# mLSTM cell and leaky-ReLU feed-forward block: q of chunk 1 through four quadrants, x by five plain transposes, two weight combinations at another place

## The chip, the cores and the metric

The kernel runs on one core of a Trainium2 chip. The metric is the device time of one execution in microseconds (us), the median over several runs. A core has a matrix engine (TensorE; in the profile PE for its matmuls and PEld for its weight loads), VectorE (DVE), ScalarE (ACT), GpSimd (POOL) and SyncE (SP, which here only issues DMAs). The engines run side by side, each in its own order, and wait for each other by semaphores. Matmuls read the on-chip memory SBUF and write to the accumulator memory PSUM; GpSimd works on SBUF alone.

## The reference

An mLSTM cell for 4 batches, 8 heads, 768 tokens and a head dimension of 40, whose output of shape (3072, 320) goes through a feed-forward block with 2048 hidden units:

```python
for t in range(S):
    m_new = np.maximum(f_gate[:, :, t] + m, i_gate[:, :, t])
    f_stab = np.exp(f_gate[:, :, t] + m - m_new)
    i_stab = np.exp(i_gate[:, :, t] - m_new)
    m = m_new
    C = f_stab * C + i_stab * np.einsum('bhd,bhe->bhde', vt, kt)
    n = f_stab * n + i_stab * kt
    h_tilde = np.einsum('bhde,bhe->bhd', C, qt)
    denom = np.maximum(np.abs(np.einsum('bhd,bhd->bh', n, qt)), 1.0)
    y[:, :, t] = sigmoid(o_gate[:, :, t]) * h_tilde / denom
x = y.transpose(0, 2, 1, 3).reshape(3072, 320)
h = x @ w_in                      # (3072, 2048)
out = np.maximum(0.01 * h, h) @ w_out
```

## The kernel before

**Tiling.** The 768 tokens are cut into six chunks of 128 (c = 0 to 5), and a step s = 4c + b is one chunk of one batch b with its 8 heads. The recurrence becomes, for each step, a masked score product of k and q inside the chunk and a product of q with the state S carried over. Chunk 0 is computed in its whole length (`u_transpose`, `u_scores`, `u_values`, `gate`). From chunk 1 on each step is cut into two halves of 64 tokens, which lie on partitions 0 to 63 and 64 to 127. The feed-forward block runs in groups g = 0 to 5 of 512 tokens, one chunk of all four batches; group 0 is computed plainly (`ff_units`, tiles `ph` at line 804 and `po` at line 826), the groups from 1 on by a scheme of seven products on sums and differences of blocks of the operands (`fast_firsts` with `ph` at line 977, `fast_units` with `po` at line 861), for which such sums of w_in (`sums_of_weights`), of w_out (`mixed_weights`) and of x (`sums_of_x`) are made once or per group.

**Order of the work.** TensorE, VectorE, ScalarE and GpSimd run in the order in which the program was written out: first `first_chunk`, then a loop over c = 1 to 6, in which the units of feed-forward group c - 1 (index i) are interleaved by hand with the cell units of chunk c: `place` and `pairs` say behind which i a cell unit stands, and single lines such as `if c == 1 and i >= 24: run(sums, 3)` place other work. SyncE issues its DMAs in an order of its own.

**A step of chunk 1** (s = 4 to 7; `u_parts`, then `u_plain`). `u_split` has put k and q, transposed, into `kqT` by way of the PSUM tiles `tk` (line 581), whose matmuls against the identity go through all four pairs of a row half and a column half. `prep_qs` has multiplied q by its gate on GpSimd (`qs`, in a tile named `y`, line 523). `split_qs` transposes `qs` by matmuls against the identity into two PSUM tiles `tq` (line 567): head by head, token half 0 to the upper output rows and token half 1 to the lower. ScalarE copies each tile into `qn` (line 569, 40 partitions x 512). Then come the scores `sd` (line 662) with the state's increments (line 667), VectorE's product with the weights `w` into `qn` (line 672) and its addition to the state S (`state_add`, line 643). `w` is made by ScalarE's exponentials (line 494) of what GpSimd masked (line 486). `u_plain` multiplies `qn` by S into `hN` (line 710); VectorE and GpSimd form x from it (lines 721 and 726), and `ahead` then prepares the next step (`tk`, `qs` by line 523, `vu` by line 514, the next mask).

**x to its transposed form.** In chunks 0 and 1 `u_x` transposes x (128 tokens x 320) into `xT`, which has five slots of 128 partitions, each with two blocks of 64 columns: the slots hold columns 0 to 127, 128 to 255, then the pair of 256 to 319 and 0 to 63, then 64 to 191 and 192 to 319. Four slots come from transposes of 128 columns (tile `xt`, line 789); the middle one from two matmuls of 64 columns against the identity, one for each half of the output rows (tile `xe`, line 791). Three copies bring them to `xT` (lines 792 to 794). In chunk 0 the last copy of every second step is VectorE's (`on_v`). Chunk 0's x comes from `gate` (lines 695 and 699), and between its steps stand GpSimd's memsets of `prepare_step` (lines 178 to 180) and the widening of w_in from 64-bit words (`narrow_weights`, lines 272 to 281). From chunk 2 on x goes through DRAM (`u_mix`, `x_dr`, `gather_x`) and does not pass `u_x`.

**Gates.** `gates(c)` runs short scans on VectorE over 32 rows; from chunk 1 on it subtracts the running maximum from the input gate into a tile `il` of its own (lines 299 and 300). `load_fi` brings the gates of a later chunk into one of two buffers `fi`.

**Combinations of w_out.** `mixed_weights` makes four combinations of quarters of w_out on VectorE, one per `next` (lines 224 to 227): t3 = a22 - a12, then a12 is overwritten by a12 - a11, then t2 and t4 from that. They are used by `fast_units` of group 1 for the first time (units 14 and up): t4 by p4, t2 by p6, t3 by p7, a12 by p5. The first two stand at the end of group 0, the other two in group 1 at i = 11 and 12. In group 1 units 0 to 13 are those of `fast_firsts`; p5's bank is used further by p3.

Of the kernel before, what the change touches and what calls it, by code (L numbers as in the profile page):

```python
# [19 lines left out]
def kernel(  # L20
# [28 lines left out]
    P = 128  # L49
# [6 lines left out]
    D1 = D + 1  # L56
    QW = 32
    DB = D // 2
    V1 = DB + 1
    TB = P // QW  # L60
    SL = P // 2
# [228 lines left out]
    def gates(c):  # L290


        m0 = m0s.get(c)
        n = P if c == 0 else BH
        fc, il = (f0[:], i0[:]) if c == 0 else (fi[c][:, 0, :], fi[c][:, 1, :])
        F = wk.tile([n, P], F32, name="F", bufs=1)
        nc.vector.tensor_tensor_scan(F[:], fc, zeros[:n].to_broadcast([n, P]), 0.0, op0=ALU.add, op1=ALU.add)
        if c > 0:
            il_t = wk.tile([BH, P], F32, name="il", bufs=1)
            nc.vector.tensor_scalar(il_t[:], il, scalar1=m0[:], scalar2=None, op0=ALU.subtract)  # L300
            il = il_t[:]
        m = wk.tile([n, P], F32, name="m", bufs=1)
        nc.vector.tensor_tensor_scan(m[:], fc, il, -1e30 if c == 0 else 0.0, op0=ALU.add, op1=ALU.max)
        a = early[:, 2, :] if c == 0 else wk.tile([n, P], F32, name="a", bufs=1)
        nc.vector.tensor_tensor(a[:], F[:], m[:], op=ALU.subtract)
        bu = wk.tile([n, 3, P], F32, name="bu", bufs=1)
        nc.vector.tensor_tensor(bu[:, 0, :], il, F[:], op=ALU.subtract)
        if c + 1 < NB:
            m1 = wk.tile([BH, 1], F32, name="m0")
            if c == 0:  # L310
                nc.vector.tensor_copy(m1[:], m[:BH, P - 1 :])
            else:
                nc.vector.tensor_tensor(m1[:], m0[:], m[:, P - 1 :], op=ALU.add)
            m0s[c + 1] = m1
        if c > 0:
            na = wk.tile([BH, 1], F32, name="na")
            nc.vector.tensor_tensor(na[:], m[:, SL - 1 : SL], F[:, SL - 1 : SL], op=ALU.subtract)
        bus[c] = bu, a, (na if c > 0 else None)
# [243 lines left out]
    def split_qs(s):  # L562

        tq = [psc.tile([P, H, SL], F32, name=f"tq{u}", tag="c") for u in range(2)]
        for h in range(H):
            for u, toks, rows in subs(s):
                nc.tensor.matmul(tq[u][rows, h, :], lhsT=st[s]["qs"][toks, h], rhs=ident[toks, toks], start=True, stop=True)  # L567
        for u, toks, rows in subs(s):
            nc.scalar.copy(mixed(s)[rows, u], tq[u][rows])

    def u_split(s):

# [117 lines left out]
    def gate(s):  # L690

        d = st[s]
        d["x"] = wk.tile([P, Dm], F32, name="x")
        x3 = d["x"][:].rearrange("p (h d) -> p h d", d=D)
        nc.vector.scalar_tensor_tensor(
            x3, in0=d["o"].rearrange("p (h d) -> p h d", d=D), scalar=1.0, in1=d["pa"][:, :, :D],
            op0=ALU.add, op1=ALU.mult,
        )
        nc.vector.tensor_tensor(x3, x3, d["den"][:].unsqueeze(2).to_broadcast([P, H, D]), op=ALU.mult)

    def u_plain(s):

# [11 lines left out]
        state_next(s, 1)  # L714
        den = wk.tile([P, H], F32, name="den")
        denominators(den[:], hN[:, :, 0, DB])
        if b < 2:
            d["x"] = wk.tile([P, Dm], F32, name="x")[:]
        else:
            d["x"] = wk.tile([P, H, D1], F32, name="hn")[:].rearrange("p h d -> p (h d)")[:, :Dm]  # L720
        nc.vector.scalar_tensor_tensor(
            d["x"].rearrange("p (n d) -> p n d", d=DB), in0=natural(s, 2).rearrange("p h (k d) -> p (h k) d", d=DB), scalar=1.0,
            in1=hN[:].rearrange("p h k d -> p (h k) d")[:, :, :DB], op0=ALU.add, op1=ALU.mult,
        )
        x3 = d["x"].rearrange("p (h d) -> p h d", d=D)
        nc.gpsimd.tensor_tensor(x3, x3, den[:].unsqueeze(2).to_broadcast([P, H, D]), op=ALU.mult)
        state_add(s, 1)

    def u_mix(s):
# [48 lines left out]
    def u_x(s, last=None):  # L778

        c, b = divmod(s, B)  # L780
        d = st[s]
        if b == 0:
            st["xT", c] = wk.tile([P, KC, GT], F32, name="xT", bufs=1)
        xT = st["xT", c]
        xt = psc.tile([P, KC - 1, P], F32, name="xt", tag="c")
        xe = psc.tile([P, P], F32, name="xe", tag="c")
        x, tok = d["x"], ts(b, P)
        for n, at in enumerate((0, P, DP, DP + P)):
            nc.tensor.transpose(xt[:, n, :], x[:, at : at + P], ident[:])  # L789
        for r, at in enumerate((KF * P, 0)):  # L790
            nc.tensor.matmul(xe[ts(r, DP), :], lhsT=x[:, at : at + DP], rhs=ident[:], start=True, stop=True)
        nc.scalar.copy(xT[:, :2, tok], xt[:, :2, :])  # L792
        nc.scalar.copy(xT[:, 2, tok], xe[:])
        (last or nc.scalar.copy)(xT[:, 3:, tok], xt[:, 2:, :])
        if c > 0:
            del st[s]

# [418 lines left out]
    with tc.manual_schedule(engines={E.PE, E.DVE, E.Activation, E.Pool}):  # L1216
# [20 lines left out]
        late = {}  # L1237
        masks = {0: (2, 3), 14: (4, 5)}
        pairs = (1, 1, 3, 3, 13, 13, 17, 17, 17)
        sums = sums_of_weights()  # L1240
        N1 = 14
        now = (None for n in range(2, QN + NF // 2) for _ in narrow_weights(n))
        chores, slow = [], []
        for c in range(1, NB + 1):
# [6 lines left out]
            for i in range(n_ff):  # L1251
# [20 lines left out]
                        del fine[min(fine)]  # L1272
                if c == 1 and i >= 24:
                    run(sums, 3)
                if c == 1 and i == n_ff - 2:
                    mixes = mixed_weights()
                if c == 1 and i >= n_ff - 2 or c == 2 and 11 <= i < N1 - 1:
                    next(mixes)
                if i == n_ff - 1 and c < NB:
                    sums_of_x(c)  # L1280
# [74 lines left out]
```

## Time and profile before

| | |
|---|---|
| runs, us | 490.13, 490.45, 492.2 (median 490.45) |
| the profiled execution, us | 489.68 |
| its span, first to last instruction, us | 487.9 |
| mean granted clock of TensorE | 0.983 |
| TensorE's matmuls busy | 476.3 (98%) |
| VectorE busy | 334.8 (69%) |
| ScalarE busy | 202.8 (42%) |
| GpSimd busy | 176.3 (36%) |

In the profile L567 is line 567 of the kernel before; a group of instructions is named by its line, engine, operation, output and inputs. An fp32 matmul against weights shows as two records, a transpose as one. A window's row gives the stretch, its length, then busy time and instructions of PE, PEld, DVE, ACT and POOL, then the granted clock of TensorE (1.00 is full speed), the share of the DMA engines and GB/s. In a row of a timeline stand start, duration, engine, line, operation, shapes and count, and in brackets how long the engine had been idle and what is inferred to have released it.

### The profile page before, as it was taken

Reading aid. Unit: us, or ns where it says so; the run is one execution under the profiler, and the core shown is the slowest. Engines: PE = TensorE matmul, PEld = TensorE weight load, DVE = VectorE, ACT = ScalarE, POOL = GpSimd, SP = SyncE. Lnnn points to the kernel's source line nnn. Section 1 sums busy time; section 2 is a strip of 40 time slices with the busy share of each in tenths; the row PEclk is TensorE's granted clock in tenths of the full one; section 3 lists DMA queues with packets and bytes.
Section 4 is the critical chain, followed back from the end, with each engine's and each line's share of the span. In section 5 each row is a group of like instructions: output and inputs, shape, how many; then the busy total and the mean of one; then the engine's idle time right before and its main releaser. Section 6 shows DMA issues by size and latency. Waiting matters only on the chain.

```text
span 487.9 us, 14080 instructions
## 1 busy us (share of the span) xinstructions
PE 476.3 (98%) x5685; PEld 428.5 (88%) x5685; DVE 334.8 (69%) x557; ACT 202.8 (42%) x488; POOL 176.3 (36%) x233
## 2 busy tenths in 40 slices
PE   8798999999999999999999999999999999999997
PEld 6676998777678899989899988899989899988997
DVE  3756567699999798888687878688647677104631
ACT  3662498864335631256420345520346411153210
POOL 4311305552376222785113784113773003700020
PEclk9887899999999999999999999999999999999999
DMA  9999686878651584675763775764865212100001
GB/s 122 172 200 210 121 223 179 207 138 173 145 142 28 126 170 83 148 167 122 173 137 88 172 150 123 181 124 90 174 146 126 60 48 68 68 1 1 1 0 55
DMA packets 165040, 59.31 MB, mean 122 GB/s; under 512 B 128560, under 2 KB 155760, under 8 KB 164976
## 3 DMA queue, kind: packets, MB, share of 16 engines
q1 hardware_dynamic: 124944, 51.23, 47.3%
q10 hardware_dynamic: 40032, 7.18, 9.0%
q8 instruction: 45, 0.74, 0.6%
q14 instruction: 19, 0.16, 0.1%
HBM read 51.68 MB, written 6.70 MB: 120 GB/s over the span
## 4 chain that ended last, share of the span: by engine, by line
PE 90%; DMA 4%; SPq 4%; DVE 1%; issue 1%; ACTq 0%; ACT 0%
PE ph L977 32%; PE po L861 32%; PE po L826 7%; PE ph L804 7%; SPq L91 4%; PE pT L740 3%; PE sd L662 3%; DMA acts<-in_moe_w_in_dram 2%; DMA raw<-in_moe_w_in_dram 1%; PE sd L667 1%; PE hN L710 1%; PE tk L581 1%; PE tq L567 1%; PE xt L789 1%; DMA f<-in_f_gate_dram 0%
## 5 line engine op out<-in xcount | busy, mean ns | idle before, releaser
L861 PE MATMUL po<-w_out,acts 128*128 128x160 f32 x640 | 89.1, 300 | 0.0
L861 PEld LDWEIGHTS po<-w_out,acts 128*128 128x128 f32 x640 | 87.3, 190 | 0.6 <-ACT acts L1002 0.3
L977 PE MATMUL ph<-xT,w_in 64*128 64x256 f32 x720 | 82.7, 378 | 0.0
L977 PEld LDWEIGHTS ph<-xT,w_in 64*128 64x128 f32 x720 | 69.3, 187 | 8.8 <-issue 1.1
L1006 DVE TENSOR_TENSOR acts<-acts,ph 128x512 f32<-128x512 f32 x60 | 38.4, 683 | 43.4 <-PE ph L977 43.4
L861 PE MATMUL po<-raw,acts 128*128 128x160 f32 x480 | 66.4, 300 | 0.0
L861 PEld LDWEIGHTS po<-raw,acts 128*128 128x128 f32 x480 | 65.4, 190 | 0.3
L1010 ACT COPY acts<-ph 128x512 f32<-128x512 f32 x60 | 32.1, 586 | 49.1 <-PE ph L977 49.1
L639 POOL TENSOR_TENSOR S<-S,f 40x336 f32<-40x336 f32 x36 | 29.5, 819 | 61.2 <-PE pT L740 26.2
L1002 ACT ACTIVATE acts<-acts 128x1024 f32<-128x1024 f32 x30 | 31.7, 1056 | 44.1 <-DVE acts L1006 33.7
L486 POOL TENSOR_TENSOR w<-w,i 128x512 f32<-128x512 f32 x20 | 26.7, 1340 | 59.5 <-DMA w<-a_dr 41.3
L494 ACT ACTIVATE w<-w,gT 128x64 f32<-128x64 f32 x160 | 41.7, 339 | 10.5 <-DMA w<-a_dr 5.7
L804 PE MATMUL ph<-xT,w_in 64*128 64x256 f32 x320 | 38.5, 395 | 0.7 <-DVE w_in L281 0.7
L672 DVE TENSOR_TENSOR qn<-w,sd 64x512 f32<-64x512 f32 x40 | 27.3, 683 | 15.6 <-ACT acts L1010 4.5
L826 PE MATMUL po<-w_out,acts 128*128 128x320 f32 x128 | 37.1, 441 | 0.0
L977 PE MATMUL ph<-acts,w 64*128 64x256 f32 x320 | 36.6, 381 | 0.0
L804 PEld LDWEIGHTS ph<-xT,w_in 64*128 64x128 f32 x320 | 32.5, 196 | 4.4 <-PE dC L619 0.8
L754 POOL TENSOR_TENSOR xb<-xb,den 128x320 f32<-128x320 f32 x16 | 11.6, 727 | 61.1 <-DVE xb L751 61.1
L977 PEld LDWEIGHTS ph<-acts,w 64*128 64x128 f32 x320 | 30.4, 187 | 3.7
L826 PEld LDWEIGHTS po<-w_out,acts 128*128 128x128 f32 x128 | 23.5, 190 | 9.8 <-issue 1.0
L959 POOL TENSOR_TENSOR acts<-xT 64x256 f32<-64x256 f32 (+1 forms) x30 | 25.5, 862 | 13.0 <-ACT xT L792 9.9
L894 POOL TENSOR_TENSOR y<-y,raw 128x160 f32<-128x160 f32 x10 | 9.4, 944 | 55.8 <-DVE acts L896 45.3
(173 smaller groups left out, 780.0 us busy)
## 6 DMA issues: line engine op xcount, KB each, us to landing
rb<-in_k_dram SPq DMA_DIRECT2D x64, 80.0 KB
rb<-in_q_dram SPq DMA_DIRECT2D x64, 80.0 KB
rb<-in_o_gate_dram SPq DMA_DIRECT2D x64, 80.0 KB
ea<-a_dr SPq DMA_DIRECT2D x32, 128.0 KB
raw<-in_moe_w_out_dram SPq DMA_DIRECT2D x6, 640.0 KB
w<-a_dr ACTq DMA_DIRECT2D x24, 128.0 KB
xT<-x_dr SPq DMA_DIRECT2D x32, 96.0 KB
x_dr<-x SPq DMA_DIRECT2D x64, 40.0 KB
```

Source lines behind the costliest of these rows:

```text
L486: nc.gpsimd.tensor_tensor(w, w, cm2.unsqueeze(1).to_broadcast([P, H, SL]), op=ALU.add)
L494: yield nc.scalar.activation(w[:, h, :], w[:, h, :], AF.Exp, bias=gT[c][:, 0, bh : bh + 1], scale=1.0)
L639: nc.gpsimd.tensor_tensor(new, old, g, op=ALU.mult)
L672: nc.vector.tensor_tensor(mixed(s)[toks, u], w[toks], bank[1 - u][toks], op=ALU.mult)
L804: nc.tensor.matmul(ph[r][:, cols], lhsT=w_row(r, slot, j), rhs=xT[DP * r : DP * (r + 1), slot, cols], start=(slot == 0), stop=(slot == KC ...
L826: nc.tensor.matmul(po[n][:], lhsT=acts[:, f, ts(n, P)], rhs=w_out[:, f, :], start=(f == 0), stop=(f == NF - 1),)
L861: nc.tensor.matmul(bank[:], lhsT=left[:, f, :], rhs=right[:, f, :], start=f == 0, stop=f == KH - 1)
L959: nc.gpsimd.tensor_tensor(to, left, right, op=ALU.subtract)
L977: nc.tensor.matmul(bank[r][:, e, :], lhsT=left(r)[rows, e], rhs=right(r)[rows], start=first and e == 0 and m == 0, stop=e == 1 and m == le ...
L1002: nc.scalar.activation(to, z, AF.Prelu, alpha=0.01)
L1006: nc.vector.tensor_tensor(to[:, 2 * r : 2 * r + 2], to[:, 2 * r : 2 * r + 2], bank[r], op=ALU.add)
L1010: nc.scalar.copy(to[:, 2 * r : 2 * r + 2], bank[r])
```

## The change

Five edits come together:

1. `split_qs` takes the heads in the order 0, 4, 1, 5, 2, 6, 3, 7. Heads 0 to 3 go to the output rows they went to; heads 4 to 7 go to the other half. Each row half of the array is so used with both column halves. Four ScalarE copies of 256 columns bring the tiles to `qn` in place of two of 512.
2. `u_x` makes five transposes of 128 columns: two into `low`, three into `high`. So that the middle slot (columns 256 to 319 and 0 to 63) is one run of 128 columns, x gets a width of 384 (`XW`), and GpSimd copies its first 64 columns behind the 320, in `gate` (chunk 0) and in `u_plain` (chunk 1). Two copies per step bring the tiles to `xT`.
3. In chunk 0 this copy of step s stands on GpSimd's queue where `gate(s)` is written out, that is, ahead of the memsets of `prepare_step`.
4. The first two of the four combinations of w_out move from the end of group 0 to i = 3 and 4 of group 1.
5. The input gate is scaled in place in `fi`; the tile `il` is gone.

On TensorE, VectorE, ScalarE and SyncE the order of all other instructions stays as it was.

```diff
--- before.py
+++ after.py
@@ -56,6 +56,7 @@
     D1 = D + 1
     QW = 32
     DB = D // 2
+    XW = Dm + DP
     V1 = DB + 1
     TB = P // QW
     SL = P // 2
@@ -296,9 +297,7 @@
         F = wk.tile([n, P], F32, name="F", bufs=1)
         nc.vector.tensor_tensor_scan(F[:], fc, zeros[:n].to_broadcast([n, P]), 0.0, op0=ALU.add, op1=ALU.add)
         if c > 0:
-            il_t = wk.tile([BH, P], F32, name="il", bufs=1)
-            nc.vector.tensor_scalar(il_t[:], il, scalar1=m0[:], scalar2=None, op0=ALU.subtract)
-            il = il_t[:]
+            nc.vector.tensor_scalar(il, il, scalar1=m0[:], scalar2=None, op0=ALU.subtract)
         m = wk.tile([n, P], F32, name="m", bufs=1)
         nc.vector.tensor_tensor_scan(m[:], fc, il, -1e30 if c == 0 else 0.0, op0=ALU.add, op1=ALU.max)
         a = early[:, 2, :] if c == 0 else wk.tile([n, P], F32, name="a", bufs=1)
@@ -562,11 +561,13 @@
     def split_qs(s):
 
         tq = [psc.tile([P, H, SL], F32, name=f"tq{u}", tag="c") for u in range(2)]
-        for h in range(H):
+        for h in (0, 4, 1, 5, 2, 6, 3, 7):
             for u, toks, rows in subs(s):
-                nc.tensor.matmul(tq[u][rows, h, :], lhsT=st[s]["qs"][toks, h], rhs=ident[toks, toks], start=True, stop=True)
+                to = rows if h < 4 else slice(SL * u, SL * u + D)
+                nc.tensor.matmul(tq[u][to, h, :], lhsT=st[s]["qs"][toks, h], rhs=ident[toks, toks], start=True, stop=True)
         for u, toks, rows in subs(s):
-            nc.scalar.copy(mixed(s)[rows, u], tq[u][rows])
+            for hs, to in ((slice(0, 4), rows), (slice(4, H), slice(SL * u, SL * u + D))):
+                nc.scalar.copy(mixed(s)[rows, u, hs], tq[u][to, hs])
 
     def u_split(s):
 
@@ -690,13 +691,14 @@
     def gate(s):
 
         d = st[s]
-        d["x"] = wk.tile([P, Dm], F32, name="x")
-        x3 = d["x"][:].rearrange("p (h d) -> p h d", d=D)
+        x = d["x"] = wk.tile([P, XW], F32, name="x")[:]
+        x3 = x[:, :Dm].rearrange("p (h d) -> p h d", d=D)
         nc.vector.scalar_tensor_tensor(
             x3, in0=d["o"].rearrange("p (h d) -> p h d", d=D), scalar=1.0, in1=d["pa"][:, :, :D],
             op0=ALU.add, op1=ALU.mult,
         )
         nc.vector.tensor_tensor(x3, x3, d["den"][:].unsqueeze(2).to_broadcast([P, H, D]), op=ALU.mult)
+        nc.gpsimd.tensor_copy(x[:, Dm:], x[:, :DP])
 
     def u_plain(s):
 
@@ -714,16 +716,14 @@
         state_next(s, 1)
         den = wk.tile([P, H], F32, name="den")
         denominators(den[:], hN[:, :, 0, DB])
-        if b < 2:
-            d["x"] = wk.tile([P, Dm], F32, name="x")[:]
-        else:
-            d["x"] = wk.tile([P, H, D1], F32, name="hn")[:].rearrange("p h d -> p (h d)")[:, :Dm]
+        x = d["x"] = wk.tile([P, XW], F32, name="x" if b < 2 else "hn")[:]
         nc.vector.scalar_tensor_tensor(
-            d["x"].rearrange("p (n d) -> p n d", d=DB), in0=natural(s, 2).rearrange("p h (k d) -> p (h k) d", d=DB), scalar=1.0,
+            x[:, :Dm].rearrange("p (n d) -> p n d", d=DB), in0=natural(s, 2).rearrange("p h (k d) -> p (h k) d", d=DB), scalar=1.0,
             in1=hN[:].rearrange("p h k d -> p (h k) d")[:, :, :DB], op0=ALU.add, op1=ALU.mult,
         )
-        x3 = d["x"].rearrange("p (h d) -> p h d", d=D)
+        x3 = x[:, :Dm].rearrange("p (h d) -> p h d", d=D)
         nc.gpsimd.tensor_tensor(x3, x3, den[:].unsqueeze(2).to_broadcast([P, H, D]), op=ALU.mult)
+        nc.gpsimd.tensor_copy(x[:, Dm:], x[:, :DP])
         state_add(s, 1)
 
     def u_mix(s):
@@ -778,20 +778,15 @@
     def u_x(s, last=None):
 
         c, b = divmod(s, B)
-        d = st[s]
         if b == 0:
             st["xT", c] = wk.tile([P, KC, GT], F32, name="xT", bufs=1)
-        xT = st["xT", c]
-        xt = psc.tile([P, KC - 1, P], F32, name="xt", tag="c")
-        xe = psc.tile([P, P], F32, name="xe", tag="c")
-        x, tok = d["x"], ts(b, P)
-        for n, at in enumerate((0, P, DP, DP + P)):
-            nc.tensor.transpose(xt[:, n, :], x[:, at : at + P], ident[:])
-        for r, at in enumerate((KF * P, 0)):
-            nc.tensor.matmul(xe[ts(r, DP), :], lhsT=x[:, at : at + DP], rhs=ident[:], start=True, stop=True)
-        nc.scalar.copy(xT[:, :2, tok], xt[:, :2, :])
-        nc.scalar.copy(xT[:, 2, tok], xe[:])
-        (last or nc.scalar.copy)(xT[:, 3:, tok], xt[:, 2:, :])
+        x, xT, tok = st[s]["x"], st["xT", c], ts(b, P)
+        low = psc.tile([P, 2, P], F32, name="xt", tag="c")
+        high = psc.tile([P, KC - 2, P], F32, name="xe", tag="c")
+        for t, n, at in ((low, 0, 0), (low, 1, P), (high, 1, DP), (high, 2, DP + P), (high, 0, 2 * P)):
+            nc.tensor.transpose(t[:, n, :], x[:, at : at + P], ident[:])
+        nc.scalar.copy(xT[:, :2, tok], low[:])
+        (last or nc.scalar.copy)(xT[:, 2:, tok], high[:])
         if c > 0:
             del st[s]
 
@@ -1237,7 +1232,7 @@
         late = {}
         masks = {0: (2, 3), 14: (4, 5)}
         pairs = (1, 1, 3, 3, 13, 13, 17, 17, 17)
-        sums = sums_of_weights()
+        sums, mixes = sums_of_weights(), mixed_weights()
         N1 = 14
         now = (None for n in range(2, QN + NF // 2) for _ in narrow_weights(n))
         chores, slow = [], []
@@ -1272,9 +1267,7 @@
                         del fine[min(fine)]
                 if c == 1 and i >= 24:
                     run(sums, 3)
-                if c == 1 and i == n_ff - 2:
-                    mixes = mixed_weights()
-                if c == 1 and i >= n_ff - 2 or c == 2 and 11 <= i < N1 - 1:
+                if c == 2 and i in (3, 4, 11, 12):
                     next(mixes)
                 if i == n_ff - 1 and c < NB:
                     sums_of_x(c)
```

## The prediction

> **What bounds the kernel now.** First the page's head: span, and busy times of the engines.
>
> ```profile
> span 487.9 us, 14080 instructions
> PE 476.3 (98%) x5685; PEld 428.5 (88%) x5685; DVE 334.8 (69%) x557; ACT 202.8 (42%) x488; POOL 176.3 (36%) x233
> ```
>
> TensorE is busy 98% of the span. Then the chain of waits in order of time (start, us, what, records):
>
> ```profile
> 44.75 0.50 DVE x L699
> ...
> 47.34 1.41 DVE w_in L281
> ...
> 48.88 10.46 PE ph L804 x80
> 59.34 1.03 PE tk L581 x64
> 60.37 6.73 PE ph L804 x60
> 67.10 0.96 PE tq L567 x30
> ...
> 116.01 1.06 PE hN L710 x32
> 117.08 2.35 PE po L826 x8
> 119.43 0.44 PE xt L789 x4
> 119.86 0.37 PE xe L791 x4
> ...
> 484.87 0.32 DVE y L920
> ```
>
> Up to 48.88 other engines and DMA decide; the last to release TensorE there is VectorE's widening of w_in (L281). From 48.88 to 484.87 every piece of the chain is TensorE behind itself. So a microsecond taken out of TensorE behind 48.88 shortens the kernel by one, unless an operand is then late; before 48.88 only what delays L281, and the clock, count.
>
> **The change, part by part.** *tq in four quadrants (chunk 1, four steps).* Now 30 records take 0.96, 32 ns each, and the last two run among those of sd. The neighbour tk has 64 records of the same shape in 1.03, 16 ns each, and its order alternates two row halves and two column halves as the new order of tq does (heads 0, 4, 1, 5 and so on). At tk's pitch 32 records take 0.515. I count 0.99 for them now: a gain of 0.475 a step, 1.9 in all. Bounds: 0 (nothing more overlaps) to 4 x 0.51 = 2.0.
>
> [...]
>
> *x by five plain transposes (chunk 1, four steps).* Four transposes take 0.44, 0.11 each, and the two half-width matmuls 0.37. Five will take 0.55 in place of 0.81: 0.26 a step, 1.04 in all. Bounds: 0.9 to 1.1, as all parts of it are there. Only the fifth reads the 64 columns that GpSimd now copies behind x. In steps 4 to 6 x is ready long before 119.43; for step 7 it comes just ahead of the S addition at 123.03 (a row below), and its transposes are at 119.43 + 3 x (0.81 + 4.70) = 136. The copy, at most a 512-column memset's 0.52 (below), stands on GpSimd's queue ahead of the next y, which tq needs, and of vu, which sd needs. I cost it at nothing, since the ph or po between (6.73 ahead of the first tq) covers it and GpSimd is busy 36%; with that cover gone it would be 3 x 0.25 to 0.5. ScalarE copies xT in two pieces instead of three.
>
> *What hands time back in chunk 1.* TensorE reaches hN of step 7 (116.01) 4 x 0.475 = 1.9 earlier, at 114.11. hN needs the state S from L643. ScalarE and VectorE in steps 6 and 7:
>
> ```profile
> 88.86 2.37 ACT L587 COPY kqT<-tk 40x512 f32<-40x512 f32 x4 [1.16 <-PE tk L581]
> ...
> 95.41 1.18 ACT L569 COPY qn<-tq 40x512 f32<-40x512 f32 x2
> 96.49 0.59 ACT L494 ACTIVATE w<-w,gT 128x64 f32<-128x64 f32 x2
> ```
> ```profile
> 97.11 1.40 DVE L672 TENSOR_TENSOR qn<-w,sd 64x512 f32<-64x512 f32 x2 [3.65 <-DMA rb<-in_o_gate_dram]
> ...
> 114.69 0.50 DVE L643 TENSOR_TENSOR S<-S,sd 40x336 f32<-40x336 f32 x1
> ...
> 123.03 0.51 DVE L643 TENSOR_TENSOR S<-S,sd 40x336 f32<-40x336 f32 x1
> ```
> ```profile
> 97.10:115.20 18.10, 18.10 (x247) 13.31 (x246) 17.39 (x28) 10.35 (x22) 9.15 (x8) 1.00 0.81 158
> ```
>
> From 97.11 on VectorE is full (third pair of the last row: 17.39 of 18.10), and S of step 7 ends at 115.19. It can move up only as far as L672 of step 6 does. The DMA named there isn't what holds L672: it starts at 97.11 where w's exponentials end (96.49 + 0.59), and those close a chain on ScalarE that began behind tk of step 6. That tk moves up by two savings, 0.95. Four copies of 256 columns in place of two of 512 cost ScalarE between nothing and another 1.18; by columns it is nothing but the start-up, so I take 0.15. So S ends 0.8 earlier, and hN waits 115.19 + 0.06 - 114.11 - 0.8 = 0.35. Bounds: 0, and 1.4 where S doesn't move and GpSimd's copies slow VectorE too. The next meeting is xt of step 5 with S at 123.54: from the first meeting VectorE needs 8.35 and TensorE some 8.6 (119.86 + 0.37 + twice 2.35, less 0.26, from 116.01), so no second wait.
>
> *Two combinations of w_out moved from the end of group 0 to units 3 and 4 of group 1.*
>
> ```profile
> 136.77 1.49 DVE L224 TENSOR_TENSOR raw<-w_out 128x1280 f32<-128x1280 f32 x1
> 138.30 1.90 DVE L225 TENSOR_TENSOR w_out<-w_out 128x1280 f32<-128x1280 f32 x1
> ...
> 145.15 1.38 DVE L672 TENSOR_TENSOR qn<-w,sd 64x512 f32<-64x512 f32 x2 [0.96 <-PE sd L667]
> ...
> 166.60 1.28 DVE L1006 TENSOR_TENSOR acts<-acts,ph 128x512 f32<-128x512 f32 x2 [2.33 <-PE ph L977]
> ```
> ```profile
> 168.92 5.35 PE L977 MATMUL ph<-xT,raw 64*128 64x256 f32 x48
> ```
>
> They take 3.39. At their old place VectorE had 0.96 to spare ahead of L672, and TensorE will come 2.5 earlier: left there, L672 would be some 1.5 late; taken away, it still waits for sd. At the new place VectorE waits 2.33 ahead of p5's additions. The cover falls short by 1.06, so the additions end at 168.94 instead of 167.88, counted in the old times; p3, which writes on into p5's banks from 168.92, needs the first of them, 0.6 before that. Cost 0; where the additions run slower, up to 0.5. Ahead of them, hb of u_mix comes 1.5 later; its x is for group 2. The gate scaled in place adds no instruction; the next load into it waits for one more reader.
>
> *Chunk 0.* Here TensorE waits, so its 0.26 a step isn't counted. VectorE's copy of three blocks replaces a wait for ScalarE and a copy of two: even. But GpSimd's queue now has the copy of x(3), whose x ends at 45.25, ahead of prepare_step's six memsets, which ended at 43.07. They will run from about 45.5 to 48, under L281:
>
> ```profile
> 42.55 0.52 POOL L180 MEMSET S<- 32x512 f32 x1
> ```
> ```profile
> 47.25 1.48 DVE L281 CUSTOM_DVE_ANT_0 w_in<-acts,w_in 128x2560 uint16<-128x2560 uint16 x1
> ...
> 60.39 2.59 DVE L281 CUSTOM_DVE_ANT_0 w_in<-raw,w_in 128x2560 uint16<-128x2560 uint16 x1
> ```
> ```profile
> 21.00:28.00 7.00, 5.51 (x26) 3.89 (x28) 6.25 (x9) 4.35 (x13) 0.00 (x0) 0.52 1.21 194
> 42.00:52.00 10.00, 7.66 (x64) 6.12 (x66) 7.68 (x19) 1.55 (x5) 0.77 (x2) 0.50 0.84 169
> ```
>
> The same L281 took 2.59 at 60.39, where GpSimd's mask addition ran beside it. So its end moves by 0 to 1.1; I take 0.3, as the memsets read nothing and cover less than half of it. Up to 52 TensorE runs at half clock (granted clock 0.50 in the last row), where a delay costs half of itself: 0.15, less 0.05 for the first two x. That is 0.1; bounds -0.2 and 1.1.
>
> *Sum*: -1.9 - 1.04 + 0.35 + 0.1 = -2.5. The profiled execution took 489.68 (span 487.9), which gives 487.2. The runs shown are 490.13, 490.45 and 492.2; their median is 0.77 above the profiled one, and I add 0.5 of that: **487.7**.
>
> **Rivals.** *A, all of it arrives*: VectorE's work moves up with TensorE and hN never waits: -2.94, and chunk 0 even, 486.7 + 0.5 = 487.2. For it: step 6 is gated by ScalarE, not by a load. Against: 17.39 of 18.10.
>
> *B, VectorE paces chunk 1*: S of step 7 doesn't move, hN waits 1.4, and p3 waits 0.5: -2.94 + 1.4 + 0.5 + 0.1 = -0.9, 489.3. For it: VectorE full from 97 on. Against: step 6's start at the end of w.
>
> *D, the change doesn't do what it says*: the quadrants overlap no further, only x gains, and hN has nothing to wait for: -1.04 + 0.1 = -0.9, 489.2. Against: tk.
>
> *C, the clock, on the other side.* The two half-clock rows above cover 7 and 10 us. 80 records from 48.88 took 10.46; at full clock (6.73 for 60) they would take 8.97, so 3.1 us of half clock cost 1.49, 0.48 each. The change takes plain matmuls out of both stretches and delays ph at 48.88. If each stretch lasts half as long again, 8.5 us more cost 4.1, and with L281's full 1.1 the loss is 5.2 against a gain of 2.6: +2.6, 492.3 + 0.5 = 492.8. It decides from 5 us of additional half clock on. For it: in the second row TensorE was busy for 7.66 of 10.00 and still at half clock. Against: most of that work stays.
>
> [...]
>
> **How the numbers follow.** Forecast 0.48 (own range 486.7 to 488.7), A 0.17, B 0.08, D 0.05, C 0.22. 0.5% (2.45 us, about what a measurement of this kernel can tell from no change) below the median is 488.0, above it 492.9. Faster: A and 0.7 of the forecast, 0.51. Slower: the upper part of C, 0.14, as its price has no ceiling in these rows. Within: the rest, 0.35. The range 486.2 to 491.0 leaves out most of C and little below A.
>
> **What would show it.** Right: tq near 0.52 a step, xt and xe together 0.55, ph again released near 49, hN of step 7 with a wait under 1, L672 in group 1 still waiting for sd. Wrong: tq still near 0.96 (D); TensorE waiting for S or for L1006 by more than 1 (B); granted clock 0.50 well beyond 52, or L281 at 2 us and more (C).

## The result and the profile after

The changed kernel takes 489.69 us (median of 22 executions, 487.42 to 490.37) against 490.55 us (22 executions, 489.52 to 496.98) of the kernel before on the same chips: a ratio of 0.9968, 95% interval 0.9954 to 0.9982. That is a gain of 1.6 us by the ratio, where 2.5 had been forecast. A ratio leaves out executions more than 1.5% above the fastest of their kernel. The profiled execution took 487.76 us. Its line numbers are those of the changed kernel: ph of group 0 is L799, tq L567, tk L582, hN L712, S L644, x's transposes L787.

The 22 executions are not one group: nine lie between 487.4 and 488.9 (below, the lower group) and thirteen between 489.35 and 490.4 (the upper group). The mean granted clock was 0.976 in ten of the thirteen and in none of the nine (there 0.979 or 0.982). As an estimate from these means, spread over the span of 486 and with half clock as the only lower state (in the windows of 1 us of the changed kernel's trace, 20 to 60, the clock is 0.50 or 1.00 but for one window at an edge of a stretch), 0.982 means 17 us at half clock, 0.979 means 20 and 0.976 means 23. The profile below is one of the nine, and what it shows is not the whole of the median.

The head of its page, and the line of the page that gives the chain's shares by engine:

```profile
span 486.0 us, 14033 instructions
PE 471.8 (97%) x5661; PEld 426.0 (88%) x5661; DVE 334.1 (69%) x557; ACT 202.8 (42%) x488; POOL 180.2 (37%) x241
...
PE 82%; DMA 7%; SPq 6%; DVE 2%; ACT 1%; issue 1%; POOL 0%; ACTq 0%; POOLq 0%
```

The chain of waits of the changed kernel (start, us, what, records):

```profile
46.51 1.41 DVE w_in L282
...
48.06 7.52 PE ph L799 x40
...
78.16 1.23 POOL S L640
...
79.47 1.19 POOL vu L513
...
95.45 5.51 DMA rb<-in_q_dram
...
101.01 1.09 PE tk L582 x60
...
109.64 0.59 PE tq L567 x32
...
115.76 1.06 PE hN L712 x32
116.82 2.35 PE po L821 x8
119.17 0.22 PE xt L787 x2
119.39 0.33 PE xe L787 x3
119.72 4.31 PE po L821 x16
...
136.44 5.38 PE ph L972 x48
...
482.94 0.32 DVE y L915
```

Up to tk of step 7 the chain is no longer TensorE alone: it runs over GpSimd's vu, over loads of k, and over the load of q for step 7, which lands at 100.96 and releases tk. Behind that it is TensorE again. The single pieces came out as meant: tq 0.59 a step (0.96 before), x 0.22 + 0.33 = 0.55 (0.81 before), and po behind x 4.31 for 16 records, where it was 4.50.

Where the time came from and went, by the starts of TensorE's groups or of the chain's pieces in the two traces (before, then after):

| | before | after | difference in it |
|---|---|---|---|
| ph released at the end of chunk 0 | 48.88 | 48.06 | -0.82 |
| its 80 records | 10.46 | 11.80 | +1.34 |
| tq to the next ph or po, steps 4, 5, 6, 7 | 1.95, 1.96, 1.96, 1.95 | 1.52, 1.64, 1.89, 1.62 | -0.43, -0.32, -0.07, -0.33 |
| hN of step 6 to the next po | 2.10 | 2.46 | +0.36 |
| x of step 4 to group 1 | 19.08 | 17.27 | -1.81 |
| group 1 to the last y | 346.36 | 346.50 | +0.14 |

The differences sum to -1.94; the last y starts 1.93 earlier (484.87, 482.94).

Windows of the changed kernel at the end of chunk 0 (stretch, length, busy time and count of PE, PEld, DVE, ACT, POOL, then granted clock, DMA share, GB/s):

```profile
41.00:44.00 3.00, 1.01 (x9) 0.77 (x8) 2.63 (x7) 0.81 (x2) 0.24 (x1) 0.95 1.19 194
44.00:47.00 3.00, 2.38 (x37) 2.08 (x37) 1.52 (x3) 0.37 (x1) 2.19 (x7) 0.50 1.06 235
...
50.00:53.00 3.00, 3.00 (x18) 2.58 (x16) 1.02 (x5) 0.30 (x2) 0.00 (x0) 0.50 0.72 147
53.00:56.00 3.00, 3.00 (x26) 2.77 (x24) 0.00 (x0) 0.74 (x4) 2.44 (x3) 0.84 0.75 98
```

ph starts earlier but runs at half clock to nearly 54, where it was 52 before, and so ends later. GpSimd's six memsets ran from 44.71 to 47.03, most of them ahead of the widening of w_in (46.43 to 47.91): only their last 0.6 us ran beside it, and it took 1.41 as before.

### The profile page after: what moved, and what is told of

It reads as the page before. It is cut to its first block, busy times and chain, and to the rows that moved or that the text cites. A ratio compares the mean times of both kernels' runs of the same rounds, so it can differ in the third digit from the quotient of the medians.

```text
span 486.0 us, 14033 instructions
## 1 busy us (share of the span) xinstructions
PE 471.8 (97%) x5661; PEld 426.0 (88%) x5661; DVE 334.1 (69%) x557; ACT 202.8 (42%) x488; POOL 180.2 (37%) x241
## 4 chain that ended last, share of the span: by engine, by line
PE 82%; DMA 7%; SPq 6%; DVE 2%; ACT 1%; issue 1%; POOL 0%; ACTq 0%; POOLq 0%
PE ph L972 33%; PE po L856 32%; SPq L92 6%; PE po L821 6%; PE pT L740 3%; DMA kn<-in_k_dram 3%; PE sd L663 3%; PE ph L799 3%; DMA acts<-in_moe_w_in_dram 1%; DMA rb<-in_q_dram 1%; PE sd L668 1%; DMA qn<-in_q_dram 1%; DMA w<-a_dr 1%; DVE w_in L281 1%; DVE w_in L282 1%
## 5 line engine op out<-in xcount | busy, mean ns | idle before, releaser
L640 POOL TENSOR_TENSOR S<-S,f 40x336 f32<-40x336 f32 x36 | 31.0, 862 | 58.0 <-PE pT L740 25.4
L997 ACT ACTIVATE acts<-acts 128x1024 f32<-128x1024 f32 x30 | 31.7, 1056 | 43.1 <-DVE acts L1001 35.4
L799 PE MATMUL ph<-xT,w_in 64*128 64x256 f32 x320 | 39.7, 403 | 1.6 <-DVE w_in L282 1.6
L673 DVE TENSOR_TENSOR qn<-w,sd 64x512 f32<-64x512 f32 x40 | 27.3, 683 | 16.4 <-ACT w L493 8.7
L799 PEld LDWEIGHTS ph<-xT,w_in 64*128 64x128 f32 x320 | 33.5, 200 | 5.6 <-ACT kqT L599 1.2
```

The costliest lines, as they stand in the source:

```text
L640: nc.gpsimd.tensor_tensor(new, old, g, op=ALU.mult)
L673: nc.vector.tensor_tensor(mixed(s)[toks, u], w[toks], bank[1 - u][toks], op=ALU.mult)
L799: nc.tensor.matmul(ph[r][:, cols], lhsT=w_row(r, slot, j), rhs=xT[DP * r : DP * (r + 1), slot, cols], start=(slot == 0), stop=(slot == KC ...
L997: nc.scalar.activation(to, z, AF.Prelu, alpha=0.01)
```

## Experiments

Times are medians with their range and number; the ratio is to the kernel before on the same chip. Line numbers are those of each kernel.

### The parts alone

tq's order alone, in the kernel before (`e1_tq`: the hunk of `split_qs` from the diff, nothing else).

> The kernel before with the four-quadrant order of tq alone. Theory (tq's saving arrives in part: 0.43 + 0.32 + 0.07 + 0.33 at its four places in the changed kernel, less 0.36 where tk of step 7 waits for its load of q): 490.5 - 0.8 = 489.7, up to 490.5 - 1.15 = 489.4, all executions within 0.8 us of each other, as chunk 0 is that of before. Rival D (the quadrants bring the tq row but nothing behind it): 490.5. Rival by the prediction's own term (1.9 less a wait of 0.35): 489.0.

Measured: 489.5 (488.33 to 492.22, 12 executions), ratio 0.9981 (0.9965 to 0.9997). In its trace TensorE goes from the second run of ph (60.84, before 60.30) to group 1 (138.03, before 138.44) 0.95 faster. So the gain is there, at half the size of the term of 1.9. The four pieces from tq to the next ph or po take 1.53, 1.61, 1.53 and 1.61 here, 1.54 less than before in all; most of the rest of it is handed back in a wait of 0.41 for VectorE's hn (L723). The first half-clock stretch of this trace lasted 10.2 us (18.7 to 28.9) and in the kernel before 6.8, although chunk 0 is the same in both.

The transposes of x alone, with the gate scaled in place to make room (`e2_x`: the hunks of `gates`, `gate`, `u_plain` and `u_x`).

> The kernel before with x by five transposes alone, in chunks 0 and 1. Theory: chunk 1 gives back 1.81 (0.26 a step in xt and xe and 0.19 a step in the po behind them); chunk 0 hands back 0.52 where the clock rises as in the profile of the changed kernel, and 2.7 where it stays low for some 6 us more: two groups of times, near 489.2 and near 491.4. Rival (chunk 0 costs nothing, the 0.52 and the two groups come from elsewhere): one group near 488.7. Rival (the prediction's 1.04 for chunk 1): 489.5.

Measured: 492.63 (492.0 to 493.08, 5 executions), ratio 1.005 (1.0038 to 1.0063): slower than before, and worse than each theory. Two windows of its trace:

```profile
26.00:29.00 3.00, 2.22 (x11) 1.73 (x11) 1.96 (x2) 1.17 (x2) 0.77 (x2) 0.50 1.07 238
29.00:32.00 3.00, 3.00 (x16) 2.58 (x15) 0.00 (x0) 0.00 (x0) 0.00 (x0) 0.50 1.24 211
```

In the kernel before, the clock was back by 28.2 and the first 20 records of ph took 2.64 there. Here it stays at half to about 32, and they take 4.56 (at 27.67). That is chunk 0's loss: ph of the end starts at 50.59. In chunk 1 the 1.81 does arrive. From the start of group 1 (139.41) to the end of its ph run it then takes 37.5, where the kernel before takes 35.8 (138.44 to 174.20). There the two combinations of w_out still stand at the end of group 0 in this kernel. The next but one experiment takes that up.

### Chunk 0 as before, all else changed

In the changed kernel, `u_x` of chunk 0 keeps the four transposes, the two half-width matmuls and the three copies, and `gate` has no copy on GpSimd.

```diff
@@ def gate(s):
-        nc.gpsimd.tensor_copy(x[:, Dm:], x[:, :DP])
@@ def u_x(s, last=None):
+        if c == 0:
+            xt = psc.tile([P, KC - 1, P], F32, name="xt", tag="c")
+            xe = psc.tile([P, P], F32, name="xe", tag="c")
...
+            return
```

> The changed kernel with x of chunk 0 transposed as before (four transposes and two half-width matmuls, no copy on GpSimd), everything else changed. Theory (chunk 0 is where 0.52 and the upper group of times come from): 490.5 - 2.6 = 487.9, one group of times, mean granted clock as before, 80 ph records from about 48.9 in 10.5. Rival (the spread of the times has another origin, in chunk 1 or in the loads): two groups as in the changed kernel, median 489.7 less at most 0.5.

Measured: 487.46 (486.98 to 487.98, 5 executions), ratio 0.9945 (0.9933 to 0.9957), all below the upper group, mean clock 0.979 to 0.982. ph starts at 48.72 and its 80 records take 10.38. With chunk 0's part gone the other parts bring 2.7 us by the ratio, so that part costs the changed kernel 1.1 us in the ratio, and without it none of five executions came into the upper group, where thirteen of 22 were.

### The two combinations of w_out back at their old place

In e9_old0, the loop's lines as before:

```diff
-                if c == 2 and i in (3, 4, 11, 12):
+                if c == 1 and i == n_ff - 2:
+                    mixes = mixed_weights()
+                if c == 1 and i >= n_ff - 2 or c == 2 and 11 <= i < N1 - 1:
```

> e9_old0 with the two combinations of w_out at the end of group 0, as before the change. Theory (the prediction's step): TensorE comes 2.5 earlier to group 1, VectorE had 0.96 to spare there, so the first additions of group 1 on VectorE are 1.5 late and TensorE waits up to that: 487.5 + 1.0 to 1.5 = 488.5 to 489.0. Rival (TensorE has other work between, the move is worth nothing): 487.5, no wait of TensorE for VectorE between 135 and 152.

Measured: 490.14 (488.76 to 494.05, 10 executions), ratio 0.9995 (0.9976 to 1.0014). VectorE's timeline at the start of group 1:

```profile
138.64 1.92 DVE L225 TENSOR_TENSOR raw<-w_out 128x1280 f32<-128x1280 f32 x1
140.60 1.90 DVE L226 TENSOR_TENSOR w_out<-w_out 128x1280 f32<-128x1280 f32 x1
142.42 0.94 DVE L298 TENSOR_TENSOR_SCAN F<-fi,zeros 32x128 f32<-32x128 f32 x1
...
146.53 1.38 DVE L673 TENSOR_TENSOR qn<-w,sd 64x512 f32<-64x512 f32 x2
```

and TensorE's waits in that stretch (who, for whom: us in total, times, longest):

```profile
PE pT L739 <- DVE S L644: 1.3, 2, 0.7
```

The changed kernel's row at the same place:

```profile
143.08 1.39 DVE L673 TENSOR_TENSOR qn<-w,sd 64x512 f32<-64x512 f32 x2 [1.22 <-PE sd L668]
```

Here L673 starts 3.4 later than in the changed kernel, while TensorE reaches group 1 only 0.5 later (136.84 against 136.37). From the start of group 1 to the end of its ph run it takes 37.9 (136.84 to 174.73), in e9_old0 35.8 (135.89 to 171.65): 2.1 lost. (In this trace ph's 80 records took 11.79, with the same chunk 0 as e9_old0 and its 10.38; from that, from pa ahead of it, 4.21 in place of 3.77, and from the mean clock of 0.979 the second half-clock stretch is estimated at 13.7 us. That loss is not in the 2.1.) The kernel before, with the same old place, takes 35.8 as well. So the move is worth about 2 us once x is faster; in the kernel before nothing is lost there. Moving the two combinations alone, in the kernel before, was not tried.

### The clock at the start of chunk 0: filling 0.78 us

In the changed kernel TensorE idles 0.78 from 26.5 on, ahead of the first ph (the row at 27.29 in the next section); before the change it did not. Ahead of the transposes of step 2's q were put two matmuls of the identity, then instead three transposes of it:

```diff
+            if s == 2 and i == 1:
+                for _ in range(2):
+                    nc.tensor.matmul(tp[:, 0, :], lhsT=ident[:], rhs=ident[:], start=True, stop=True)
```
```diff
+            if s == 2 and i == 1:
+                for _ in range(3):
+                    nc.tensor.transpose(tp[:, 0, :], ident[:], ident[:])
```

> The changed kernel with two extra 128x128 matmuls on the identity (their output is overwritten) ahead of the transposes of step 2's q, so that TensorE no longer idles 0.78 ahead of the first ph at 27.2. Theory (that idle time, which x by five transposes opened, keeps the clock at half for one more stretch of some 3.4 us in most executions, and the 20 ph records take 4.56 in place of 2.43): all executions have a mean clock of 0.979 to 0.983, one group of times, median 488.0 (the lower group of the changed kernel) and up to 0.5 less. Rival (the clock's stretches begin and end by chance): median 489.7 and two groups as in the changed kernel.

> The changed kernel with three extra 128x128 transposes of the identity at the same place, for about the same time. If transposes are busy time for the clock as matmuls are: the same as with the two matmuls, one group near 488.0. [...]

Measured: with matmuls 487.34 (486.08 to 488.53, 6 executions), ratio 0.9931 (0.9911 to 0.995), mean clock 0.979 to 0.982, all below the upper group. In its trace the first ph took 2.95 for 20 records in place of 2.43, so half clock reached some 1.1 into it; with the mean clock of 0.979 and ph's 80 records at the end of chunk 0 (10.69) the first half-clock stretch is estimated at 10.2 us (19.0 to 29.3). With transposes 488.68 (486.36 to 491.58, 12 executions), ratio 0.9965 (0.9944 to 0.9986), mean clock 0.975 or 0.976 in five of the twelve, all of these above 489.8. None of six with matmuls against five of twelve with transposes is weak evidence of a difference between the two, and the profiled execution with transposes, the slowest of the twelve, lost its time elsewhere. Its chain of waits:

```profile
96.60 6.74 DMA rb<-in_q_dram
...
103.39 1.86 PE tk L582 x60
105.24 3.20 PE po L824 x8
```

and a window of it:

```profile
103.00:107.00 4.00, 3.61 (x64) 2.87 (x65) 2.95 (x6) 1.65 (x3) 3.04 (x4) 0.57 0.87 164
```

The load of q for step 7 landed at 103.3 and not at 101. TensorE waited 2.8, the clock fell, tk and po then ran at half clock (1.86 for 1.09, 3.20 for 2.35), and hN of step 6 to the po behind it took 6.00 in place of 2.10: a price of 3.9 us for a load that is 2.4 late. So an execution can be slow in two ways, and times alone don't say which it was. Whether some of the changed kernel's thirteen are of this kind stays open, as none of them was traced; but e9_old0, which comes to that load 0.75 earlier, has none in its five.

### Plain matmuls for transposes

To see whether transposes keep the clock low, the five transposes of x in chunk 0 of the changed kernel were made plain matmuls on the identity:

```diff
+            if c == 0:
+                nc.tensor.matmul(t[:, n, :], lhsT=x[:, at : at + P], rhs=ident[:], start=True, stop=True)
+            else:
                 nc.tensor.transpose(t[:, n, :], x[:, at : at + P], ident[:])
```

> The changed kernel with the five transposes of x in chunk 0 (20 in all) as plain matmuls on the identity, nothing added. [...]

Measured: 489.74 (485.23 to 492.73, 12 executions), ratio 0.997 (0.9943 to 0.9997). The median is that of the changed kernel (489.69), the clock is not: its mean reached 0.993 in the three fastest, which no kernel with transposes in all four steps of chunk 0 did (at most 0.989, in e5_swap), and was 0.976 in two of those above 491. Two windows:

```profile
47.00:50.00 3.00, 3.00 (x28) 2.77 (x30) 0.52 (x2) 0.37 (x1) 2.10 (x7) 0.51 1.04 179
50.00:53.00 3.00, 1.85 (x36) 1.76 (x34) 2.88 (x7) 0.00 (x0) 0.00 (x0) 1.00 0.51 117
```

By windows of 1 us the stretch lasted from 43.1 to 50.0, 6.8 us; in the changed kernel 43.7 to 54.0, 10.2. But in this execution half clock came once more between (36.3 to 39.7), under the second ph of chunk 0 (4.11 for 20 records, 2.43 before). And plain matmuls take longer, five of them 2.27 at half clock (x of step 0, 22.70 to 24.97) where five transposes took 1.23 (22.27 to 23.50): ph of the end of chunk 0 starts at 51.59, 3.5 later than in the changed kernel, and tk behind it at 60.42, 0.6 later. What made the other executions of this kernel slow stays open.

The changed kernel's own trace answers part of the question. TensorE's timeline at the start of chunk 0, then two windows:

```profile
22.27 0.66 PE L787 MATMUL xt<-ident,x 128*128 128x128 f32 x2 [3.14 <-DVE x L700]
...
25.44 1.06 PE L596 MATMUL tkq<-ident,qn 128*128 128x128 f32 x4
27.29 2.43 PE L799 MATMUL ph<-xT,w_in 64*128 64x256 f32 x20 [0.78 <-DVE w_in L282]
```
```profile
25.00:26.00 1.00, 1.00 (x7) 1.00 (x6) 0.97 (x2) 0.31 (x1) 0.83 (x4) 0.50 1.03 205
27.00:28.00 1.00, 0.71 (x6) 0.74 (x8) 0.61 (x2) 0.13 (x1) 0.00 (x0) 1.00 1.06 260
```

From 22.27 to 26.50 TensorE ran 18 transposes (ten of x, eight of k and q) and nothing else, all at half clock and behind 3.14 of idle time; from 26.65 on the clock was full. So here the clock came back behind transposes alone.

### Other things late, and a version that beats both

VectorE made x of step 3 behind a widening step of w_in; the two were exchanged (`e5_swap`), in the changed kernel:

```diff
         u_x(2)
+        gate(3)
         run(w, 1)
-        gate(3)
         u_x(3, on_v)
```

> The changed kernel, VectorE in another order at the end of chunk 0: x of step 3 is made ahead of the widening step of w_in that took 1.49 from 42.06, not behind it. Then x of step 3 is ready at about 43.1 and not at 44.47, its copy no longer waits 1.48, and ph starts near 46.7 and not at 48.06. Theory (TensorE's idle 2.60 ahead of x of step 3 is what lets the clock go): the half-clock stretch is shorter or gone, all times below 487.4, near 486. Rival (the clock falls anyway and stays low for some 10 us): ph starts 1.35 earlier at half clock, worth 0.7: two groups, 487.0 and 489.2.

Measured: 487.94 (486.07 to 489.1, 6 executions), ratio 0.9951 (0.9934 to 0.9969). ph starts at 49.20, but the whole end of chunk 0 is later here: from the second ph of chunk 0 (37.35; 35.29 in the changed kernel) to it are 11.85, in the changed kernel 12.77. So 0.9 of the 1.35 arrives. The rest went to GpSimd's copy of 64 columns, for which the fifth transpose now waited 0.35. The first half-clock stretch lasted 10.2 here and 6.8 in the changed kernel's trace, and the first ph took 4.57: the fault at the start of chunk 0 is still in it. The second stretch was shorter, 6.8 (45.2 to 52.1) against 10.2, with transposes in both kernels.

Then all together: chunk 0 as before, this exchange, and in chunk 1 GpSimd's copy behind the preparation of the next step:

```diff
@@ def u_plain(s):
-        nc.gpsimd.tensor_copy(x[:, Dm:], x[:, :DP])
...
                         ahead(s + 2)
+                    if fn is u_plain:
+                        x = st[s]["x"]
+                        nc.gpsimd.tensor_copy(x[:, Dm:], x[:, :DP])
```

> Three things together, apart in the trace: x of chunk 0 as before (e9_old0), x of step 3 ahead of the widening step (e5_swap), and in chunk 1 GpSimd's copy of 64 columns behind vu of the next step instead of ahead of y. Theory: the second part starts ph 1.3 earlier than e9_old0 (near 47.4) in a half-clock stretch, worth 0.65; the third takes the wait of sd for vu away in steps 5 and 6 (sd 1.12 in both in place of 1.24 and 1.48), 0.45, of which some stays behind the load of q that tk of step 7 waits for: 487.5 - 0.65 - 0.1 to 0.45 = 486.4 to 486.75. Rival for the copy (sd waits for S or y, not for the copy): sd unchanged. Rival for the order (the clock falls earlier with it): ph takes longer and the time is that of e9_old0, 487.5.

Measured: 486.17 (485.55 to 490.42, 7 executions), ratio 0.9922 (0.9895 to 0.995). GpSimd's timeline in step 6, first of the changed kernel, then of this one:

```profile
90.08 0.38 POOL L726 COPY x<-x 128x64 f32<-128x64 f32 x1
90.42 1.05 POOL L522 TENSOR_TENSOR y<-rb,gT 128x320 f32<-128x320 f32 x1
...
92.86 1.18 POOL L513 TENSOR_TENSOR vu<-kn,gT 128x320 f32<-128x320 f32 x1
```
```profile
90.32 1.18 POOL L513 TENSOR_TENSOR vu<-kn,gT 128x320 f32<-128x320 f32 x1
...
93.27 0.24 POOL L1307 COPY x<-x 128x64 f32<-128x64 f32 x1
```

TensorE reached tq of step 6 at 93.18 and 91.45. There vu ended 0.9 behind that start, in the middle of sd; here it ended within 0.05 of it. From tq to the next ph or po the four steps take 1.52, 1.61, 1.51 and 1.61: tq brings 1.57, and the copy had cost 0.42. ph at the end of chunk 0 starts at 47.09. In the profiled execution (487.13, in the upper half) much of it was handed back: 0.9 around the load of q (hN of step 6 to po 3.02 in place of 2.10), and 1.05 in group 1 (134.82 to 171.63, in e9_old0 135.89 to 171.65), where TensorE three times waited for ScalarE's copies of ph and once for VectorE's addition. So this version beats both kernels; that it beats e9_old0 is not shown, as the intervals meet.

Last, the second half-clock stretch in this version: its transposes of x in chunk 0 as matmuls, and four idle matmuls ahead of the state sums of step 3; then the same for steps 2 and 3 alone.

```diff
-                nc.tensor.transpose(xt[:, n, :], x[:, at : at + P], ident[:])
+                nc.tensor.matmul(xt[:, n, :], lhsT=x[:, at : at + P], rhs=ident[:], start=True, stop=True)
...
+        if s == B - 1:
+            for _ in range(4):
+                nc.tensor.matmul(dC[:].rearrange("p j k d -> p (j k d)")[:, :P], lhsT=ident[:], rhs=ident[:], start=True, stop=True)
```

> e11_combined with the four transposes of each x of chunk 0 as plain matmuls on the identity, and four extra 128x128 matmuls (overwritten) ahead of the state sums of step 3, where TensorE idles 0.67. [...]

> e14_mm_combined with plain matmuls for x of steps 2 and 3 alone; x of steps 0 and 1 by transposes as in e11_combined. In e14_mm_combined the eight plain matmuls of steps 0 and 1 took 2.05 a step at half clock in place of 1.09 and started the first ph 1.6 later (29.07, e11_combined 27.44). Theory: the first stretch is that of e11_combined, x of step 3 starts near 43.7, and the clock comes back one or two stretches earlier than 51.5 because matmuls stand where transposes stood: 80 ph records from about 47.3 in 9.0 to 9.7. TensorE reaches chunk 1 up to 2 earlier than in e11_combined, and hands part of it back at the load of q for step 7, which came no earlier than 99.9 in e14_mm_combined (wait 0.46 in e11_combined, up to 2 here), and in group 1, where VectorE and ScalarE paced e11_combined: 485.0 to 486.2. Rival (the clock needs more than that and the second stretch is 10 us): as e11_combined, 486.2, or 0.2 above it.

Measured: 488.12 (485.33 to 490.95, 12 executions), ratio 0.9958 (0.9934 to 0.9981); and 488.24 (485.44 to 492.4, 12 executions), ratio 0.9959 (0.9935 to 0.9982). Windows of the first, then of the second:

```profile
44.00:47.00 3.00, 2.66 (x37) 2.15 (x37) 2.65 (x5) 1.55 (x5) 0.12 (x1) 1.00 1.05 229
47.00:50.00 3.00, 2.79 (x38) 2.58 (x38) 2.88 (x6) 0.00 (x0) 0.00 (x0) 1.00 1.00 166
```
```profile
44.00:47.00 3.00, 3.00 (x30) 2.76 (x28) 1.01 (x3) 1.18 (x4) 0.00 (x0) 0.50 1.06 239
47.00:50.00 3.00, 3.00 (x44) 2.64 (x42) 2.88 (x6) 0.00 (x0) 0.00 (x0) 0.96 0.76 126
```

The clock comes back earlier in both, as e15_mm_late's theory has it: the second stretch is gone in one and 6.8 us long (40.4 to 47.2) in the other, and ph's 80 records take 8.90 in both. The reason need not be that matmuls stand where transposes stood. Four plain matmuls take 2.05 at half clock where four transposes took 1.09, and four idle matmuls were added, so that TensorE also stands idle for less of this time. The time does not follow: TensorE now reaches tk of step 7 at 97.85 and 98.16. In the first, tk waits 1.74 for the load of q, the clock falls there instead, and group 1 starts at 136.91; in the second (an execution of 485.44) q was there, and it starts at 133.97. What made the slower half of these executions slow was not traced.

### What a visit to the half-width mode costs

In the kernel before, x's pair of half-width matmuls made twice in each step of chunk 1; the output is the same.

> The kernel before with the pair of half-width matmuls of x made twice in each step of chunk 1 (the second writes the same again); only the trace is read. From the start of one x to the start of the next it took 5.31, and 4.86 with five transposes; a pair thus cost 0.56 beside a transpose's 0.11. If the going into the half-width mode and out of it costs something once: the second pair costs 0.2 to 0.3, cycle 5.5 to 5.6. If each half-width matmul costs 0.28 by itself: cycle 5.87.

The chain of this kernel (one execution, 491.67):

```profile
120.51 0.44 PE xt L789 x4
120.94 0.59 PE xe L792 x8
121.53 4.50 PE po L827 x16
126.03 0.44 PE xt L789 x4
```

From x to x it takes 5.52, before 5.31 (119.43 to 124.74). A second pair costs 0.21. The first cost 0.45 + 0.11 = 0.56 beside the transpose that replaced it, so 0.35 of it is paid once a visit.

## Why the prediction was right or wrong

**The forecast.** 487.7 was the time of the profiled execution (487.76) and of the lower nine, not of the median, 489.69. That lies inside the range, a little above rival B's and rival D's times. The likeliest outcome, faster by over 0.5%, did not come: it is 0.32%. That the profiled execution met 487.7 is in part luck: tq brought 0.75 less than its term and x in chunk 1 0.77 more.

**What bounds the kernel.** "A microsecond taken out of TensorE behind 48.88 shortens the kernel by one, unless an operand is then late": the second half of that sentence decided much. The time taken out made vu late in step 6 and q in step 7, and in e11_combined ScalarE's copies of ph in group 1, none of which the prediction had priced; the additions at the start of group 1 it had priced and met by the move.

**tq, -1.9 forecast, -1.15 measured.** The mechanism was right: 32 records in 0.59 (0.515 forecast), and rival D fell. The step that failed is "I cost it at nothing, since the ph or po between (6.73 ahead of the first tq) covers it": GpSimd's copy ahead of y and vu cost 0.42 by e11_combined, 0.38 of it in step 6 alone, and e1_tq, which has no copy, gains 1.54 at these four places. With the cover gone the prediction had 3 x 0.25 to 0.5, which is more than was paid. The remaining 0.33 of the 1.9 is the row's 0.59 in place of 0.515, and sd in steps 5 and 7, which took 0.09 longer than in steps 4 and 6.

**x in chunk 1, -1.04 forecast, -1.81 measured.** Mis-sized, outside its bounds of 0.9 to 1.1. The prediction counted xt and xe, where 0.26 a step came as forecast, and took the po behind for fixed; the 0.19 a step by which po fell is, by e13_pair, part of the price of a visit to the half-width mode. "All parts of it are there" was true of the records and not of what they do to their neighbours.

**hN of step 7, +0.35 forecast.** No wait there. TensorE came to it 0.25 earlier, not 1.9, and S, which ended at 115.22 and so no earlier than before, was in time. Nor was there a wait in e11_combined, where TensorE came 1.8 earlier (114.14): S ended at 113.65 there, 1.5 earlier and not 0.8. So the term was too high in either case. Two pieces of it the runs put otherwise: ScalarE's four copies, for which it took 0.15, took 1.54 in step 6 (95.21) where two had taken 1.18; and the 0.06 from S to hN stands beside no row (from the end of x's L699 at 45.25 to xt it is 0.13). In its place tk of step 7 waited 0.36 for the load of q, which the prediction had not named: it looked at VectorE (17.39 of 18.10) and not at the loads of 81 to 101.

**The combinations of w_out, 0 forecast, 0 measured.** Right, and for its reason: L673 waits 1.22 for sd at the new place, and with the old place 2 us are lost. The forecast of 1.5 for that was near.

**Chunk 0, +0.1 forecast, +0.52 in the profiled execution and about 2 more in the upper group.** This is the step that made the median. "Here TensorE waits, so its 0.26 a step isn't counted" is where it failed. The time taken out became 0.78 of idle time ahead of the first ph. Three traces have it without anything put in: in e2_x and e5_swap half clock lasted so far into ph that its 20 records took 4.56 and 4.57, in the changed kernel 2.43; in the traces without it they took 2.43 to 2.95. e9_old0 without that part has no execution in the upper group, nor has e6a_fill_mm, which fills the idle time with matmuls. So chunk 0's part is what the median lacks, about 1.1 us by e9_old0, whose interval just touches the changed kernel's. That it works by the idle time is likely, and not shown by itself: no execution of the upper group was traced, and with transposes in the idle time (e6b_fill_tr) five of twelve still had the low clock. Rival C, at 0.22, had the right mechanism, more half clock, with too high a price: the ten executions at 0.976 have 3 to 6 us more of it than those at 0.979 and 0.982, not 8.5, and that took most of the gain without turning the sign. Its other half, the widening slowed by the memsets, was hardly put to the test: 1.41, with 0.6 of memsets beside it.

**The clock and transposes.** Whether transposes keep the clock low, the runs don't decide. In the changed kernel's first stretch TensorE ran 18 transposes and nothing else (22.27 to 26.50), and the clock came back. With matmuls in place of transposes the second stretch fell from 10.2 us to 6.8 in e10_mm and e15_mm_late and to none in e14_mm_combined, but plain matmuls also keep TensorE busy for longer (2.27 for five, 1.23 for five transposes, both at half clock), and it was 6.8 in e5_swap with transposes. What a stretch needs to end stays open.

## What to carry to other kernels

Work that TensorE does while it waits for others is not free to remove where the granted clock is low (chunk 0's part costs the changed kernel 1.1 us by e9_old0; that it does so through the idle time is likely, not shown): look at the granted clock around the place, and at the idle time that opens there. When several savings in a row lie on one engine, add them up and ask at each later meeting what is late at the summed time, the loads and the smallest copy on another queue included; a piece moved away for a later meeting (the combinations of w_out) had nothing to win in the kernel before and is worth 2 us with the rest. And a few half-width matmuls among full-width ones are dear by the visit, not by their number: 0.35 a visit here, 0.21 a pair.

## What the runs showed of the hardware

- The half-clock stretches come in steps of some 3.4 us: 6.8 and 10.2 in most traces, 3.4 behind the late load of q, 13.7 in e2_x (18.4 to 32.0) and, estimated from ph's 80 records (11.79 and 11.78) and the mean clock (0.979), in e8_mixes_back and e13_pair. The last two have the chunk 0 of before, whose own stretches were 6.8 and 10.2, so a stretch's length differs between executions of the same work; the changed kernel's times fall into groups 2 us apart.
- Behind an idle time of 2.8 us in a stretch of full load came one such step (from 103.5 in e6b_fill_tr), and behind one of 1.7 as well in e14_mm_combined (from 100.1). Behind waits for the same load of 0.3 in e9_old0 and 0.5 in e11_combined came none.
- In the changed kernel the clock came back (26.65) behind 18 transposes with no matmul between them, 4.2 us at half clock (22.27 to 26.50).
- In the kernel before, VectorE's widening of w_in took 1.48 with GpSimd idle (at 47.25) and 2.59 with GpSimd's mask addition beside it (at 60.39).
